# Which engine issues the first loads: the two heads of a unit from one DMA queue or from two

## The chip, the cores and the metric

The kernel runs on one core of one Trainium2 chip. A core has five engines with instruction streams of their own: TensorE (PE, matrix products; its weight loads are shown apart as PEld), VectorE (DVE), ScalarE (ACT), GpSimd (POOL) and SyncE (SP), which here only issues transfers. They meet through semaphores. Transfers between the memory of the chip and the core's working memory (SBUF) are done by 16 DMA engines; an engine's stream only issues them. What is measured is the device time of one execution in microseconds (us), and less is better. The kernel before was timed in twelve executions: median 558.64 us, from 556.56 to 561.17.

## The reference

Two blocks follow one another. The first is a gated linear recurrence over 768 tokens, for 4 batches and 8 heads of width 48; the second mixes tokens and channels with a Fourier transform, normalises, and puts a two-layer network on top:

```python
f = 1 / (1 + exp(-f_logit))
for t in range(S):                       # per batch and head
    state = f[t, :, None] * state + k[t, :, None] * v[t, None, :]
    y[t] = q[t] @ state
x = y with the heads side by side        # (4, 768, 384)
u = x + real(fft(fft(x, axis=tokens), axis=channels))
out = u + relu(layernorm(u) @ w_ch1) @ w_ch2      # 384 -> 1536 -> 384
```

The arrays q, k, v and f_logit are inputs in float32. The weights w_ch1 and w_ch2 come as float64, and the kernel makes single precision of them on the chip.

## The kernel before

**Units.** The recurrence is done for two heads at a time. Such a pair of heads of one batch is a *unit*; there are 16, numbered u = 0 to 15, four for each batch. The channels of the pair lie on the partitions: the first head (r = 0) on partitions 0 to 47, the second (r = 1) on 64 to 111, the 768 tokens along the free axis. The rows between are filled once by a memset (`gap` on DVE for q and k, line 131; `start` on POOL for g, lines 136 to 145). Three tiles g0 to g2 hold the gate logits in turn, three tiles k0 to k2 the keys, and four tiles q0 to q3 the queries, so unit 3 takes g0 and k0 again once unit 0 has read them.

**Loads.** `load(u, names)` (line 159) issues them. For each of f, k and q it issues two transfers of 48 rows with 3072 bytes each (144 KB), one for each head, second head first, at line 170, and for v one of 288 KB at line 166. All of these go out on SP. They, the weight blocks (`words`, line 267, 384 KB each, tile raw) and the identity matrix (line 872) stand in one queue in the order of the program. The framework gives every transfer one of eight completion semaphores in turn, so a transfer also waits until the one eight places before it has landed. A tile that is used again adds a wait for its readers.

**A unit's work** is cut into steps by the generator `attention` (lines 330 to 368) and `outputs` (506 to 566):

- ACT: exp and ln of the gate logits g, in place (330, 331)
- DVE: the running sum W of these (a scan, 337) and the sums at the chunk ends (338); POOL copies the last of them (339)
- ACT: g = exp(-W), W = exp(W), and te for the chunk ends (342 to 345)
- DVE: q times g, W times k (349, 350)
- PE: the scores sc (361); DVE masks them into at (368)
- PE turns W (506), ACT copies that to kT (508), PE makes the chunk states ds from kT and v (517), DVE scans them into stt (525)
- PE: y from at and v (537), and from q and stt (544); ACT copies y to yT (553 to 557), PE turns it (564), ACT writes x (566)

**Weights.** A block comes as pairs of words. ACT converts the low word in place (238), DVE shapes the high one (240, 241), and POOL adds the two (242).

**The order** is written out by hand in the string ORDER: a number is the next step of that unit, L2q a load, r the fetch of a weight block, C its conversion, G a gap memset, I and Z POOL's memsets, D four products on constant data on PE (line 153) that keep it busy. Each engine carries out its own part of this order, strictly in sequence. Later letters (F, P, H, W) are the Fourier transform and the network, which PE is full with from about 70 us on. The order begins:

```python
ORDER = (
    "Gq2 r I D Gq0 L0f Gk1 L1f D Gk0 L0q i D Gq3 C Gq1 Z L0k 0 D 1 Gk2 0 L1q 1 L1k D 0 0 1 0 r 1 L2f 0 2 "
    "C L1v 1 L3fk D 1 3 L0v 0 1 L2q 2 0 0 r D 1 L2k 3 1 0 2 r 3 L3q 2 L2v D 0 C L3v D C L4fk R D 4 2 2 3 "
```

So the load of unit 2's gate logits (L2f) stands behind several steps of units 0 and 1, and the first step of unit 2 follows it almost at once.

At the end of the kernel, behind a test that is not met with these inputs, stands a second, slower way through the whole computation; it calls `load` too.

Of the kernel before, what the change touches and what calls it, by code (L numbers as in the profile page):

```python
# [53 lines left out]
def kernel(  # L54
# [13 lines left out]
    nc = tc.nc  # L68
# [10 lines left out]
    ROWS = [slice(64 * r, 64 * r + D) for r in range(2)]  # L79
# [79 lines left out]
    def load(u, *names):  # L159
        if u >= B * HP:  # L160
            return
        b, hp = divmod(u, HP)
        for name in names:
            if name == "v":
                v_of[u] = p3.tile([128, NCH, 2 * D], F32, tag="v", name=f"v{u}")
                nc.sync.dma_start(out=v_of[u], in_=v[b, hp])
                continue
            t, i = {"f": (g_t[u % 3], 2), "k": (k_t[u % 3], 1), "q": (q_t[u % 4], 0)}[name]
            for r in (1, 0):
                nc.sync.dma_start(out=t[ROWS[r]], in_=qkf[b, hp, r, :, i])  # L170

    def tables():

# [201 lines left out]
    def attention_by_blocks(u, x_all):  # L375
# [114 lines left out]
        T = double(64, T)  # L490
        yield
        load(u + 3, "f")
        yield from outputs(u, x_all, AT, Q, K, None, T)
        load(u + 3, "k")

    def outputs(u, x_all, AT, Q, K, te, T=None):
# [61 lines left out]
        if te is None:  # L558
            load(u + 4, "q", "v")
# [415 lines left out]
```

## Time and profile before

| | us |
|---|---|
| median of twelve executions | 558.64 |
| lowest, highest | 556.56, 561.17 |
| the profiled execution | 558.71 |
| its span, first to last instruction | 556.9 |
| PE busy | 528.2 |
| DVE busy | 299.7 |
| ACT busy | 192.7 |
| POOL busy | 95.8 |

The profile is that of one execution. Times in it count from its first instruction, and 1.8 us of the execution's time lie around the span. "Chain" is the work that ended last, followed back from the last instruction: at each step to what released it. "Idle before" is the time in which an engine had nothing it could do ahead of an instruction, with what ended it. A load's issue is short (0.3 to 0.5 us on SP); the transfer itself lands microseconds later, which the trace shows in the increments of its completion semaphore. The TensorE clock is granted in steps; 1.00 is full speed.

### The profile page before, as it was taken

What the parts mean: (1) busy time and instruction counts of PE and PEld (TensorE: products, weight loads), DVE (VectorE), ACT (ScalarE), POOL (GpSimd) and SP (SyncE); (2) the same over time, 40 slices, a digit from 0 to 9 for tenths busy, and PEclk for the clock granted to TensorE, in tenths of its full rate; (3) what the DMA queues carried; (4) which work ended last, traced back from release to release, by engine and by line L of the source; (5) the groups of instructions that cost most, each with busy time, mean ns of one, the idle gap of its engine ahead of it and who ended that gap; (6) DMA issues with size and microseconds to landing.
All of it is one profiled execution on the core that took longest, in us unless ns stands there. A gap on an engine that the chain in (4) does not pass through costs nothing.

```text
span 556.9 us, 10217 instructions
## 1 busy us (share of the span) xinstructions
PE 528.2 (95%) x4194; PEld 462.9 (83%) x4194; DVE 299.7 (54%) x534; ACT 192.7 (35%) x497; POOL 95.8 (17%) x147
## 2 busy tenths in 40 slices
PE   3988599999999999999999999999999999999995
PEld 2877478885889889889889899899889798989985
DVE  8999899994945626445554443453443342413231
ACT  6766476573313433443240331321421302121110
POOL 6146642634101000140200000103001000010000
PEclk9698989999999999999999999999999999999999
DMA  8969736453402010310730401102012005000001
GB/s 223 261 184 234 204 92 172 128 146 105 115 1 58 15 44 2 115 44 22 220 114 15 114 1 55 32 1 87 1 28 86 0 2 171 0 29 0 29 2 34
DMA packets 18398, 44.38 MB, mean 80 GB/s; under 512 B 3109, under 2 KB 4710, under 8 KB 18342
## 3 DMA queue, kind: packets, MB, share of 16 engines
q1 hardware_dynamic: 17094, 39.89, 26.0%
q0 software_dynamic: 1104, 3.54, 1.8%
q8 instruction: 35, 0.57, 0.5%
q14 instruction: 21, 0.17, 0.1%
q10 hardware_dynamic: 144, 0.20, 0.1%
HBM read 38.90 MB, written 4.72 MB: 78 GB/s over the span
## 4 chain that ended last, share of the span: by engine, by line
PE 86%; DMA 5%; DVE 4%; ACT 2%; POOL 1%; issue 1%; SPq 0%; ACTq 0%; DVEq 0%; POOLq 0%
PE up L750 34%; PE fx L773 15%; PE fz L773 12%; PE z L650 4%; PE sc L361 3%; PE po L759 3%; PE mix L669 3%; PE y L537 3%; PE y L544 3%; DMA raw<-in_w_ch_dram 2%; DMA g<-in_qkf_dram 2%; PE ds L517 2%; PE pt L708 1%; PE yt L564 1%; DMA v<-in_v_dram 1%; PE st L506 1%
## 5 line engine op out<-in xcount | busy, mean ns | idle before, releaser
L750 PE MATMUL up<-unT,w 128*128 128x256 f32 x864 | 197.1, 382 | 1.5 <-DVE x L728 0.9
L750 PEld LDWEIGHTS up<-unT,w 128*128 128x128 f32 x864 | 160.9, 190 | 26.1 <-issue 1.5
L752 ACT ACTIVATE h<-up 128x256 f32<-128x256 f32 x144 | 55.2, 383 | 200.3 <-PE up L750 194.0
L617 POOL DMA_INDIRECT out_dram<-x,place x16 | 16.9, 1059 | 270.3 <-DVE x L803 234.4
L773 PE MATMUL fx<-block,h 128*128 128x192 f32 x264 | 46.5, 326 | 0.0
L773 PE MATMUL fx<-w,h 128*128 128x192 f32 x264 | 44.9, 327 | 0.1
L773 PEld LDWEIGHTS fx<-w,h 128*128 128x128 f32 x264 | 43.1, 190 | 0.8 <-ACT h L752 0.4
L773 PEld LDWEIGHTS fx<-block,h 128*128 128x128 f32 x264 | 43.5, 190 | 0.0
L780 DVE TENSOR_TENSOR s<-h,h 128x768 f32<-128x768 f32 x11 | 10.5, 954 | 50.6 <-ACT h L752 50.6
L242 POOL TENSOR_TENSOR w<-w,raw 128x384 uint32<-128x384 uint32 x24 | 28.9, 1210 | 50.6 <-ACT raw L238 24.1
L361 PE MATMUL sc<-q,W 48*64 48x128 f32 x768 | 28.5, 299 | 6.8 <-DVE W L350 5.3
L368 DVE COPY_PREDICATED at<-causal,sc 128x768 f32<-128x768 uint32 x32 | 31.5, 1029 | 3.4 <-PE sc L361 3.3
L361 PEld LDWEIGHTS sc<-q,W 48*64 48x64 f32 x768 | 24.2, 148 | 10.8 <-DVE W L350 5.8
L337 DVE TENSOR_TENSOR_SCAN W<-g,bound 112x768 f32<-112x768 f32 x16 | 28.4, 1775 | 1.3 <-PE st L506 0.9
L725 DVE TENSOR_TENSOR x<-mix,x 128x384 f32<-128x384 f32 x12 | 6.7, 555 | 39.4 <-PE mix L669 39.4
L537 PE MATMUL y<-at,v 128*64 128x128 f32 (+1 forms) x384 | 24.5, 276 | 0.0
L773 PE MATMUL fz<-w,s 128*128 128x192 f32 x132 | 23.5, 328 | 0.0
L773 PE MATMUL fz<-block,h 128*128 128x192 f32 x132 | 23.5, 328 | 0.0
L773 PE MATMUL fz<-w,h 128*128 128x192 f32 x132 | 23.4, 327 | 0.0
L537 PEld LDWEIGHTS y<-at,v 128*64 128x64 f32 (+1 forms) x384 | 20.9, 130 | 2.9 <-issue 2.8
L153 PE MATMUL y<-bound 128*128 128x256 bf16 x92 | 15.4, 318 | 8.1 <-ACT yT L557 4.2
L773 PEld LDWEIGHTS fz<-w,s 128*128 128x128 f32 x132 | 21.6, 190 | 0.3 <-issue 0.3
(145 smaller groups left out, 742.2 us busy)
## 6 DMA issues: line engine op xcount, KB each, us to landing
raw<-in_w_ch_dram SPq DMA_DIRECT2D x24, 384.0 KB, 4.3
g<-in_qkf_dram SPq DMA_DIRECT2D x32, 144.0 KB, 4.7
q<-in_qkf_dram SPq DMA_DIRECT2D x32, 144.0 KB, 4.8
k<-in_qkf_dram SPq DMA_DIRECT2D x32, 144.0 KB, 4.4
v<-in_v_dram SPq DMA_DIRECT2D x16, 288.0 KB, 5.4
k<-in_w_ch_dram SPq DMA_DIRECT2D x12, 384.0 KB
g<-in_w_ch_dram SPq DMA_DIRECT2D x12, 384.0 KB, 5.2
out_dram<-x SPq DMA_DIRECT2D x4, 168.0 KB
```

Of the source, the lines that this page charges most:

```text
L242: nc.gpsimd.tensor_tensor(bits, bits, lo, ALU.add)
L337: nc.vector.tensor_tensor_scan(W, g, bound[:R], 0.0, ALU.add, ALU.min)
L361: nc.tensor.matmul(ps[64 * s:64 * s + 64, r, i * C:(i + 1) * C], lhsT=W[ROWS[r], o + 64 * s:o + 64 * s + 64], rhs=Q[ROWS[r], o:o + C], sta ...
L368: nc.vector.copy_predicated(AT[:, :, half], causal.bitcast(U32).unsqueeze(1).unsqueeze(1).to_broadcast([128, 2, NCH // 2, C]), ps[:, :, :N ...
L537: nc.tensor.matmul(y[FILL[r], c * C:(c + 1) * C], lhsT=vt[:, c, r * D:r * D + (64 if r == 0 else D)], rhs=AT[:, r, c], start=(c % 4 == 0), ...
L544: nc.tensor.matmul(y[ROWS[r], c * C:(c + 1) * C], lhsT=st[ROWS[r], :, c - 1], rhs=Q[ROWS[r], c * C:(c + 1) * C], start=False, stop=True, s ...
L617: nc.gpsimd.indirect_dma_start(out=out.rearrange("b s d -> (b s) d"), out_offset=bass.IndirectOffsetOnAxis(ap=place[:, b, i:i + 1], axis=0 ...
L650: nc.tensor.matmul(z[:, cols], lhsT=src[:, j, lo:hi], rhs=tab[:, t, T % 2, cols], start=(i == 0), stop=(i == len(parts) - 1), skip_group_c ...
L669: nc.tensor.matmul(mix[:, o], lhsT=zz[:rows_of[T], T, PLACES[c]], rhs=cd[:rows_of[T], T, :NQ - odd], start=(i == 0), stop=(i == 1))
L750: nc.tensor.matmul(pp[:, :256], lhsT=w1[:, kt, m * 128:(m + 1) * 128], rhs=unT[:, kt], start=(kt == 0), stop=(kt == 2))
L752: nc.scalar.activation(hs[-1][:, m % H].rearrange("p t n -> p (t n)"), pp[:, :256], AF.Relu)
L773: nc.tensor.matmul(out, lhsT=h[:, m], rhs=blocks[i][:, m], start=(start and m == 0), stop=(m == H - 1), skip_group_check=True)
```

## The change

Of the two transfers that load f, k or q of a unit, the one for the first head (r = 0) is issued by ACT instead of SP, for the units 0, 1 and 2. For units 3 to 15 both stay with SP, as do v, the weights and the constants. These are nine transfers of 144 KB. They stand in ACT's instruction stream at the places where `load` is called in ORDER.

```diff
             t, i = {"f": (g_t[u % 3], 2), "k": (k_t[u % 3], 1), "q": (q_t[u % 4], 0)}[name]
             for r in (1, 0):
-                nc.sync.dma_start(out=t[ROWS[r]], in_=qkf[b, hp, r, :, i])
+                queue = nc.scalar if r == 0 and u < 3 else nc.sync
+                queue.dma_start(out=t[ROWS[r]], in_=qkf[b, hp, r, :, i])
```

## The prediction

> **What bounds the kernel now.** I read four views, in this order: the page's head, the chain that ended last, the timeline of ScalarE (ACT) where the moved loads will stand, and the sums by stage.
>
> ```profile
> span 556.9 us, 10217 instructions
> PE 528.2 (95%) x4194; PEld 462.9 (83%) x4194; DVE 299.7 (54%) x534; ACT 192.7 (35%) x497; POOL 95.8 (17%) x147
> q1 hardware_dynamic: 17094, 39.89, 26.0%
> q10 hardware_dynamic: 144, 0.20, 0.1%
> PE 86%; DMA 5%; DVE 4%; ACT 2%; POOL 1%; issue 1%; SPq 0%; ACTq 0%; DVEq 0%; POOLq 0%
> ```
>
> TensorE is the bound, but not of the stage that is changed. Its waits after 68 us are small; of the 28.7 us that it is idle, 19.5 lie before 70 us (sums by stage). q10 is ACT's DMA queue: 144 packets, one store at the very end. So no load runs beside SP's queue (q1) in this trace.
>
> The nine moved loads all go out in the first 17 us. The chain there:
>
> ```profile
> 0.81 4.16 DMA raw<-in_w_ch_dram
> 6.09 1.01 POOL w L242
> 7.10 2.63 POOL at L214 x2
> 10.94 0.71 POOL deep L339
> 11.67 0.84 ACT W L343
> ...
> 20.36 0.95 PE st L506 x5
> 21.39 1.77 DVE W L337
> ...
> 23.27 0.75 DVE stt L525
> 24.02 1.66 DVE W L337
> 25.90 0.85 ACT g L342
> ```
>
> It runs from the first weight block through POOL's fills to ACT and VectorE (DVE), and has no load of a unit in it between 5 and 41 us. What is late in these rows is late at 41 us too: the pieces follow one another with gaps of some 0.04 us. From 41.5 to 66 us it goes over SP's loads, which start when computing frees their tiles, and from 68.5 us over TensorE. I find no slack further on that would take a delay back.
>
> How tight the loads stand to their readers is seen on ACT and in the sums by stage (columns: stage, busy time by engine, granted clock, DMA share, GB/s):
>
> ```profile
> 14.47 0.48 ACT L345 ACTIVATE te<-deep,low 112x240 f32<-112x240 f32 x1
> 14.86 0.83 ACT L330 ACTIVATE g<-g 112x768 f32<-112x768 f32 x1
> 18.05 0.84 ACT L331 ACTIVATE g<-g 112x768 f32<-112x768 f32 x1
> 21.33 0.63 ACT L508 COPY kT<-st 128x560 f32<-128x560 f32 x1 [2.44 <-PE st L506]
> ```
>
> ```profile
> 2.00:3.00 1.00, 0.00 (x0) 0.00 (x0) 0.89 (x2) 0.10 (x1) 0.94 (x3) 1.00 0.72 160
> 3.00:4.00 1.00, 0.06 (x1) 0.07 (x2) 0.89 (x2) 0.00 (x0) 0.94 (x6) 1.00 1.09 390
> 5.00:10.00 5.00, 3.39 (x16) 2.11 (x14) 4.28 (x7) 4.10 (x8) 3.93 (x8) 1.00 1.05 262
> ```
>
> The DMA engines are full from 5 us on (share 1.05). The trace's completion increments put the landings of g0 at 5.45 and 6.01, of g1 at 6.57 and 7.09, of q0 at 7.53 and 8.15: one half head pair per 0.54 us, against an issue every 0.46 us on SP. The transfers set the pace, not SP. ACT reads g2 at 14.86, and its second half had landed at 14.72.
>
> **The change, part by part.** It removes nine DMA issues from SP and adds nine to ACT: the rows 0 to 47 of g, q and k for units 0, 1, 2. Bytes, tiles and all arithmetic stay. The order of TensorE, DVE and POOL is the same in both builds; ACT's becomes (r0 is the moved half):
>
> ```
> table load, g0 r0, g1 r0, q0 r0, raw0, k0 r0, exp/ln g0, exp/ln g1, q1 r0, k1 r0,
> exp W0 and te0, exp W1 and te1, g2 r0, exp/ln g2, raw1, exp/ln g3, kT0, kT1, q2 r0, k2 r0, exp W2 ...
> ```
>
> *SP loses nine issues*: 9 x 0.46 = 4.1 us of a queue that is ahead of the transfers; I take a gain of 0. The cover is the transfer pace; were it gone, 4.1 us would be the ceiling. What SP is moved past (k, raw1, g2's other half) starts sooner but has readers that need both halves or come much later (raw1's at 17.5 us). The loads of unit 3 still wait for DVE at 12.78.
>
> *g0, g1, q0 at the start.* On SP they stood at 1.75, 2.67 and 3.60. On ACT they follow the table load (0.81 to 2.09), so from about 2.1: no later. But they now move beside raw0, the head of the chain, instead of behind it. If raw0 keeps its precedence the cost is 0; if all three (432 KB) get ahead of it, 3 x 0.54 = 1.6 us. raw0's first packets ran 0.9 us after its issue, so ACT's begin near 3.0, when by the stage rows 0.18 of raw0's 0.39 MB has been moved. I assume even sharing of the rest: 0.21 MB more in between, at the 390 GB/s of that microsecond, 0.55 us. I take **+0.6** (0 to 1.6). g0's other half is late by about as much, and POOL, ACT and DVE with it.
>
> The Trainium skill speaks to this on "DMA: Bandwidth & Descriptors", section "Queues, rings and completion order": each DMA engine alternates between the rows that have work, a packet from each. By that rule the sum holds the 0.6; by first come, first served, it would hold 0. This trace shows no two load queues at once, so it can't say. The same page's section "Issuing engines are not separate DMA queues" speaks against any gain: a second issuing engine saves issue time alone.
>
> *k0, q1, k1.* k0 r0 goes out near 5.7 (SP: 5.53) and is read at 12.67: 0. q1 and k1 wait in ACT's queue behind ln g1 and go out between 8.8 and 10 instead of 6.89 and 7.71. Read at 13.66 and 14.60, they have 4 us or more, and loads issued then landed in 3.6 to 5.5. I take 0, at most 0.6. Their two issues stand ahead of exp W0's first half (9.99), whose successor waits for POOL until 11.67: 1.7 us of cover against 0.9.
>
> *g2, the costly one.* On SP its second half was issued at 9.20, on ACT it can't be before te1, that is 14.5 to 14.95, and its reader is the next instruction. ACT then waits for the whole flight. Flights of such a load: 2.60 is the shortest in the whole trace, the ones issued on SP around then took 3.6 to 4.8 (g at 12.78: 3.58; q at 15.00: 4.83). An empty queue of its own should beat SP's backlog; I take 3.7, landing at 18.65. Bounds: 14.47 + 2.60 = 17.1, 14.95 + 4.83 = 19.8. Queued behind this wait are exp and ln of g2, raw1, exp and ln of g3 (14.86 to 18.89: 4.03 us) and then kT0, which began at 21.33 because it waited for TensorE. So 2.44 us of ACT's idle time covers: kT0 begins at 18.65 + 4.03 = 22.7, **1.35 late** (0 to 2.5). kT0 is waited for by TensorE's ds (22.16), that by DVE's stt (23.27). From kT0's start to ds is 0.83, and ds takes 0.76 at full clock: ds ends at 24.3, stt starts **1.1 late** (0 to 2.2). Behind stt on DVE stands the scan of unit 3, behind that ACT's exponentials, yT and TensorE's next block at 29.05. DVE's scan of W2 (21.39) is not touched: ln g2 ends at 20.4. A raw1 that is converted late reaches POOL at 20.4 instead of 18.6; POOL is idle until 23.2.
>
> *q2, k2.* Issued on ACT after kT1, about 24, instead of 15.47 and 16.93; read at 26.45 and 27.30, now some 1.7 later. With 3.7 of flight they land near 27.7 and 28.1: 0; with the 5 to 8 us that SP's queue showed at that time, one to three late, but the scores that read them began at 30.08 behind yT, which covers 1.8. I take 0 (0 to 1.0). Their two issues, 0.9 us if ACT stops for them, lie ahead of exp W2, which has more cover than that from unit 3's scan.
>
> *The granted clock* is not the change's, but moves with it: TensorE runs at 0.50 from 12.27 to 22.51 and from 66.88 to 73.71, in steps of 3.41 us. One step more or less over full work is 3.41 x 0.5 = 1.7 us. I take 0 (-1.7 to +1.7).
>
> **Sum.** 0.6 + 1.1 = 1.7 us onto the profiled execution: 556.9 of span and 1.8 around it, 558.7, which is the median of the twelve runs (558.64) to 0.1. So **560.4 us**.
>
> **The rivals.**
> 1. *Hidden*: raw0 keeps its precedence, and g2 lands by 17.3 (flight 2.6 with an empty queue, issue run ahead of te1). Then kT0 is on time: **558.7**. For it: 2.44 us of cover on ACT, the shortest flight. Against it: DMA engines full until 30 us.
> 2. *Worse*: the flight is 4.8 or more because the engines are full, ACT stops for its issues, and q2/k2 come late as well: 1.6 + 2.2 + 0.9 = 4.7, **563.4**. For it: flights of 5 to 8 us on SP between 15.5 and 22. Against it: those queued behind SP's own raw blocks.
> 3. *Faster*: the clock. The work that meets 70.29 to 73.71 is TensorE's 3.42 us at half rate. If the shift puts the busy stretch so that one step fewer is slow, 1.7 us fall away; with a shift under 0.6 the result is **557.0 to 557.6**. It decides only where g2's wait is covered, too. For it: the step before it holds 1.78 us of work in 3.41, so not much is missing. Against it: a shift can as well lose a step.
> That SP's freed time brings the transfers forward is not among them: they are full, and the chain holds none of the first loads but raw0.
>
> **How the numbers follow.** My case 0.47, own range 559.8 to 562; hidden 0.24; worse 0.15; faster 0.14. The range goes from rival 3's upper end to just short of rival 2's full sum: **557.5 to 563.0**, which leaves half of either, some 0.15, outside. A measurement here tells 0.2% (1.1 us) from no change: faster 0.14, same 0.24, slower 0.62.
>
> **What would show it.** In the changed kernel's profile: q10 with nine loads more; on ACT a wait for DMA g at unit 2's exp, ending near 19, 3 to 4 us long, and none there would favour the first rival; raw0 landing near 5.5, not 4.97; kT0 near 23.2 and TensorE's block of 29.05 near 30.7; everything from 68 us on shifted alike. I am wrong if ACT's own queue flies in under 2.6 us, if a shift is there at 30 us and gone at 68, or if the clock's steps differ in number.

## The result and the profile after

The changed kernel takes 563.38 us (median of 12, from 560.37 to 565.35), the kernel before, timed beside it, 558.23 (49 executions). The ratio is 1.0084, with a 95% interval from 1.0067 to 1.0100: **slower by 4.7 us** (3.7 to 5.6). The forecast was slower, with 560.4 in a range from 557.5 to 563.0; the median lies 0.4 above that range, and 558.23 and the 4.7 of the ratio, 562.9, lie just inside it. One more execution on record, 567.12, is not among the twelve. The profiled execution took 563.63, 4.9 more than that of before.

From the page of the changed kernel:

```profile
span 561.4 us, 10216 instructions
PE 528.5 (94%) x4194; PEld 462.9 (82%) x4194; DVE 300.4 (54%) x534; ACT 192.8 (34%) x497; POOL 95.7 (17%) x147
q1 hardware_dynamic: 16518, 38.57, 25.3%
q10 hardware_dynamic: 720, 1.52, 1.2%
PE 83%; DMA 6%; DVE 4%; ACT 2%; POOL 2%; issue 1%; SPq 0%; DVEq 0%; ACTq 0%; POOLq 0%
```

576 packets, nine loads of 64, have gone from q1 to q10. No engine's busy time grows by more than 0.7 us (DVE); TensorE has become idle for longer, and the chain holds more DMA. Where, the chain shows, cut to its first 45 us (columns: start, length, what):

```profile
0.81 4.41 DMA raw<-in_w_ch_dram
...
12.00 0.84 ACT W L344
...
14.10 4.45 DMA g<-in_qkf_dram
18.58 0.94 ACT g L331 x2
...
21.78 0.85 ACT g L332
22.63 0.78 ACT kT L509 x2
23.45 7.59 DMA k<-in_qkf_dram
...
31.16 0.96 DVE W L351
32.12 0.28 DVE w L241
...
34.49 1.96 DVE at L369 x2
```

(The lines of the kernel are one higher than before.) Two transfers now stand in it that were not there: unit 2's gate logits, issued at 14.10, and its keys, issued at 23.45, each directly behind the ACT work that keeps the issue back. The timeline of ACT shows that:

```profile
14.05 0.84 ACT L344 ACTIVATE W<-W 112x768 f32<-112x768 f32 x1
14.10 0.38 ACTq L171 DMA_DIRECT2D g<-in_qkf_dram  x1
14.80 0.48 ACT L346 ACTIVATE te<-deep,low 112x240 f32<-112x240 f32 x1
18.58 0.84 ACT L331 ACTIVATE g<-g 112x768 f32<-112x768 f32 x1 [3.30 <-DMA g<-in_qkf_dram]
22.53 1.18 ACT L509 COPY kT<-st 128x560 f32<-128x560 f32 x2
23.09 0.32 ACTq L171 DMA_DIRECT2D q<-in_qkf_dram  x1
23.45 0.43 ACTq L171 DMA_DIRECT2D k<-in_qkf_dram  x1
```

ACT runs on while it issues: the load of g2 goes out while exp W1 is running. What costs is not the issue but its place. On DVE, first in the kernel before, then in the changed one:

```profile
26.45 0.93 DVE L349 TENSOR_TENSOR q<-q,g 112x768 f32<-112x768 f32 x1
27.30 0.95 DVE L350 TENSOR_TENSOR W<-W,k 112x768 f32<-112x768 f32 x1
...
29.42 0.56 DVE L241 SCALAR_TENSOR_TENSOR w<-raw,w 128x384 uint32<-128x384 uint32 x1
30.96 2.00 DVE L368 COPY_PREDICATED at<-causal,sc 128x768 f32<-128x768 uint32 x2 [0.99 <-PE sc L361]
```

```profile
14.76 0.96 DVE L350 TENSOR_TENSOR q<-q,g 112x768 f32<-112x768 f32 x1 [0.81 <-DMA q<-in_qkf_dram]
...
22.41 1.76 DVE L338 TENSOR_TENSOR_SCAN W<-g,bound 112x768 f32<-112x768 f32 x1 [0.86 <-PE st L507]
...
24.29 0.75 DVE L526 TENSOR_TENSOR_SCAN stt<-ds,te 112x288 f32<-112x288 f32 x1
...
29.48 0.96 DVE L350 TENSOR_TENSOR q<-q,g 112x768 f32<-112x768 f32 x1 [1.93 <-ACT W L344]
31.16 0.96 DVE L351 TENSOR_TENSOR W<-W,k 112x768 f32<-112x768 f32 x1 [0.73 <-ACT raw L239]
32.04 0.35 DVE L241 TENSOR_SCALAR w<-raw 128x384 uint32<-128x384 uint32 x1
...
33.30 1.27 DVE L242 SCALAR_TENSOR_TENSOR w<-raw,w 128x384 uint32<-128x384 uint32 x1
34.49 1.96 DVE L369 COPY_PREDICATED at<-causal,sc 128x768 f32<-128x768 uint32 x2
```

In the same profile, on POOL:

```profile
33.13 1.02 POOL L243 TENSOR_TENSOR w<-w,raw 128x384 uint32<-128x384 uint32 x1 [6.19 <-ACT g L331]
```

DVE first waits 0.81 us for q1 (the line at 14.76) and is some 1.0 us late from there to stt. Of unit 2, the two waits that are put down to ACT were ended by the loads: the completion counts have q2's first head landing at 29.40 and k2's at 31.04, each 0.1 us before the instruction that reads it. The mask is 3.53 us late, the next TensorE blocks up to 3.5 (the turning of W at 42.51 instead of 39.03), and TensorE's last product ends at 554.31 instead of 550.42, 3.89 late. The rest of the 4.9 us, 1.0, lies behind that last product, where nothing of the change runs: from there to the end of the execution it is 9.32 us (7.05 to the end of the span, 2.27 around the span), and 8.29 before.

The landings of the loads that matter, from the issues and completion counts of the trace:

```
                       before (SP)               after (ACT)
                 issued  landed  flight    issued  landed  flight
g2, first head     9.20   14.72    5.52     14.10   18.55    4.45
q2, first head    15.47   20.59    5.12     23.09   29.40    6.31
k2, first head    16.93   24.62    7.69     23.45   31.04    7.59
```

### The profile page after: what moved, and what is told of

It reads as the page before. It is cut to its first block, busy times and chain, and to the rows that moved or that the text cites. A ratio compares the mean times of both kernels' runs of the same rounds, so it can differ in the third digit from the quotient of the medians.

```text
span 561.4 us, 10216 instructions
## 1 busy us (share of the span) xinstructions
PE 528.5 (94%) x4194; PEld 462.9 (82%) x4194; DVE 300.4 (54%) x534; ACT 192.8 (34%) x497; POOL 95.7 (17%) x147
## 4 chain that ended last, share of the span: by engine, by line
PE 83%; DMA 6%; DVE 4%; ACT 2%; POOL 2%; issue 1%; SPq 0%; DVEq 0%; ACTq 0%; POOLq 0%
PE up L751 34%; PE fx L774 15%; PE fz L774 12%; PE z L651 4%; PE po L760 3%; PE mix L670 3%; PE y L545 2%; PE sc L362 2%; PE y L538 2%; DMA raw<-in_w_ch_dram 2%; DMA wave<-in_dim_tab_dram 2%; PE pt L709 1%; PE ds L518 1%; DMA k<-in_qkf_dram 1%; PE yt L565 1%
## 5 line engine op out<-in xcount | busy, mean ns | idle before, releaser
L545 PE MATMUL y<-q,stt 48*48 48x128 f32 x320 | 21.9, 281 | 0.0
```

What stands on the lines that cost most here:

```text
L545: nc.tensor.matmul(y[ROWS[r], c * C:(c + 1) * C], lhsT=st[ROWS[r], :, c - 1], rhs=Q[ROWS[r], c * C:(c + 1) * C], start=False, stop=True, s ...
```

## The experiments

All twelve kernels were timed in five rounds beside the kernel before, with twelve executions each, but seven of e9, ten of e10 and eleven of e12. The times below are the ratio times the time of before in the same set, with the 95% interval; a single profile is used for what waits for what. How far a single profile can stray is told under the last pair.

| kernel | moved to ACT | us against before |
|---|---|---|
| the change | all nine | +4.7 (3.7 to 5.6) |
| e1 | units 0 and 1 | +0.4 (-0.4 to 1.2) |
| e2 | g2 | +0.8 (-0.3 to 2.0) |
| e3 | q2, k2 | +0.4 (-0.4 to 1.2) |
| e4 | none; q2, k2 late on SP | +2.6 (1.3 to 3.8) |
| e5 | all nine, unit 2's early | +1.7 (0.7 to 2.6) |
| e6 | none; more filler on TensorE | -1.5 (-2.6 to -0.3) |
| e7 | g2, q2, k2 | +2.8 (1.7 to 3.9) |
| e8 | units 0, 1 and g2 | +2.1 (0.8 to 3.3) |
| e9 | units 0, 1 and q2, k2 | +4.7 (3.0 to 6.4) |
| e10 | all nine, v3 on SP later | +4.7 (3.2 to 6.2) |
| e11 | none; 18 in the way that is not taken | -0.3 (-1.2 to 0.5) |
| e12 | all nine, none in the way that is not taken | +3.6 (2.5 to 4.7) |

**e1, only the units 0 and 1.**

```diff
-                nc.sync.dma_start(out=t[ROWS[r]], in_=qkf[b, hp, r, :, i])
+                queue = nc.scalar if r == 0 and u < 2 else nc.sync
+                queue.dma_start(out=t[ROWS[r]], in_=qkf[b, hp, r, :, i])
```

> Only the six first-head loads of units 0 and 1 on ACT, unit 2 back on SP. Theory Late (a load costs what its issue comes later on ACT than on SP, as far as its reader has no cover): raw0 lands near 5.2, q1's first head is issued near 9.3 and lands near 14.6, unit 1's product is some 1.0 late and the stt of unit 0 with it; exp of g2 and the products of unit 2 wait for no load. Total +0.9 us (0.4 to 1.3). Theory Queue (a transfer on ACT's queue is slow or slows SP's, wherever it stands): two thirds of the 4.7, +3.1. Theory Hold (ACT itself stands still for each issue): up to 6 x 0.4, +2.4, with a gap of 0.4 on ACT at each issue.

Measured: 558.61, +0.4, not to be told from nothing. raw0 lands at 4.58 with three loads of ACT beside it; before it was 4.97, and in kernels without them 4.74 and 4.92 (e4, e3). So the loads beside raw0 don't hold it back, and six loads in a second queue cost little by themselves, 1.2 us at most.

**e2 and e3, unit 2's parts by themselves.**

```diff
+                queue = nc.scalar if r == 0 and u == 2 and name == "f" else nc.sync   # e2
+                queue = nc.scalar if r == 0 and u == 2 and name != "f" else nc.sync   # e3
```

> Only the first head of g2 on ACT, eight loads back on SP. Late: issued near 13.8, lands near 18.2, exp of g2 waits 3 to 4 us as in the changed kernel, stt of unit 0 is 0.7 to 1.0 late, unit 2's products wait for nothing else: +1.0 us (0.5 to 1.3). Queue: one ninth of 4.7, +0.5. Hold: +0.4.

> Only the first heads of q2 and k2 on ACT. Late: issued near 22.4 and 22.8 behind the two kT copies, landing near 28.5 and 29.5 to 30, W times k of unit 2 at some 29.7 instead of 27.3, of which 1.0 us is covered by DVE's idle time ahead of the mask: +1.2 to +2.2 us. Queue: two ninths of 4.7, +1.0. Hold: +0.8.

Measured: 558.01 and 558.13, +0.8 and +0.4, both compatible with nothing. That was the surprise: q2 and k2 go out at 22.37 and 22.79 in e3, hardly sooner than in the change. The waits of SP's queue, in e2 and then in e3, from 10 to 35 us, tell what else happened:

```profile
SPq L171 <- DMA g<-in_qkf_dram: 4.3, 1, 4.3
```

```profile
SPq L166 <- DMA q<-in_qkf_dram: 7.5, 2, 7.1
```

The loads take the completion semaphores in turn, over both queues. In e2, SP's load of q2 (second head) got the semaphore that ACT's late g2 had, and was held for 4.3 us, until g2 landed at 19.82. In e3, SP's load of v3 (288 KB) was held for 7.1 us behind q2, and SP issued nothing between 20.77 and 28.24. So nothing new of SP's came beside k2; its flight was 5.78 instead of 7.59, it landed at 28.57 instead of 31.04, and the mask came 1.5 us late instead of 3.5. The edit of a part had changed the order of the rest. e2's profile doesn't look like a kernel that loses 0.8: its mask is at 34.40, 3.44 late, on a chain that starts with g2. That execution took 561.60, where the twelve go from 556.79 to 561.83; more on this under the last pair.

**e4, the same lateness without ACT.** The loads of q2 and k2 (first head) stay on SP, but stand behind q3, v2 and v3 there. They go out at 20.77 and 22.33, some 1 to 2 us sooner than from ACT in the change, and land about as late, at 30.12 and 30.77.

```diff
-    "C L1v 1 L3fk D 1 3 L0v 0 1 L2q 2 0 0 r D 1 L2k 3 1 0 2 r 3 L3q 2 L2v D 0 C L3v D C L4fk R D 4 2 2 3 "
+    "C L1v 1 L3fk D 1 3 L0v 0 1 L2q 2 0 0 r D 1 L2k 3 1 0 2 r 3 L3q L2v L3v s2q s2k 2 D 0 C D C L4fk R D 4 2 2 3 "
...
+                late = n == 2 and word in ("L2q", "L2k")
+                load(n, *word.strip("L0123456789"), heads=(1,) if late else (1, 0))
+            elif kind == "s":
+                load(n, *word.strip("s0123456789"), heads=(0,))
```

> Nothing on ACT: all loads on SP, but the first heads of q2 and k2 stand behind q3, v2 and v3 in SP's queue, so that they are issued near 21 and 22. Late: they land near 29.2 and 29.7, behind everything issued before, and the cost is that of the kernel with both on ACT, +1.0 to +2.0 us. Queue and Hold: 0, since ACT issues nothing.

Measured: 560.09, +2.6. Its chain between 18 and 36 us:

```profile
20.77 9.35 DMA q<-in_qkf_dram
...
30.22 0.58 DVE q L349
...
31.09 0.96 DVE W L350
...
32.15 2.84 PE sc L361 x48
```

The mask is 3.44 late, as in the change, with not one load on ACT. So neither a second queue nor ACT's issuing is needed for this part of the loss: a late place in the order of the loads is enough.

**e5, all nine on ACT, but unit 2's earlier in ACT's order.**

```diff
-    "... L1q 1 L1k D 0 0 1 0 r 1 L2f 0 2 "
+    "... L1q 1 L1k a2f D 0 0 1 0 r 1 L2f a2q 0 2 a2k "
...
+            elif kind == "a":
+                load(n, *word.strip("a0123456789"), heads=(0,))
```

In this kernel the load of a first head goes to ACT for u < 3, as in the change.

> All nine first-head loads on ACT as in the changed kernel, but unit 2's stand further ahead in ACT's stream: g2 behind k1 (issue near 10), q2 ahead of exp g2 (near 14 to 15), k2 behind ln g2 (near 17). Late: g2 is there when exp g2 is reached, q2 and k2 land by 21 and 25, the wait at unit 2's products is gone; what is left is raw0 (+0.3) and q1 (+0.8): +0.5 to +1.2 us. Queue: +4.7, as the changed kernel. Hold: +3.6.

Measured: 560.39, +1.7 instead of +4.7. The three loads now go out at 9.62, 13.53 and 16.91, and the mask is 0.67 late. The nine loads on ACT's queue by themselves are not what costs; 1.7 is left, and of this the end of the kernel has about 0.9 (below).

Of the three theories that the expectations of e1 to e5 set against each other, Late (the loads go out late because of their place in the program) is the one that holds, by e4 and e5. Queue (two load queues are in each other's way) falls with e1, e4 and e5; Hold (the issues stop ACT's own work) falls with e1, e4 and the timeline of ACT above.

**e6, more filler on TensorE in the kernel before.** Five more words D stand ahead of the first scores, 20 products on constant data.

```diff
-    "... L0k 0 D 1 Gk2 0 L1q 1 L1k D 0 0 1 0 r 1 L2f 0 2 "
+    "... L0k 0 D 1 Gk2 0 L1q 1 L1k D D D D D D 0 0 1 0 r 1 L2f 0 2 "
```

> The kernel before with twenty more of TensorE's filler products (line 153) ahead of the first scores, all loads on SP. If the granted clock's step is worth what the prediction's third rival said, 1.7 us for 3.4 us of full work, the filler up to 12.8 takes the half-rate stretch of 12.27 to 22.51 away or shortens it, the scores of units 0 and 1 take 1.5 us each instead of 2.8, and 1 to 2.5 us fall away. If the stage is bound by DVE, which is busy in 0.97 of every microsecond from 8 to 19, it is 0 to -0.7 us.

Measured: 557.04, ratio 0.9973 (0.9953 to 0.9994), 1.5 us faster than before. It is the fastest of all kernels here. Granted clock (behind the busy times) from 12 to 23 us and in three later stretches, in before and in e6:

```profile
12.00:23.00 11.00, 9.28 (x130) 8.05 (x130) 9.93 (x11) 7.99 (x14) 1.02 (x1) 0.53 1.04 251
46.00:50.00 4.00, 3.82 (x55) 3.21 (x56) 3.05 (x6) 1.49 (x3) 1.77 (x2) 0.57 1.03 236
57.00:65.00 8.00, 5.09 (x90) 4.20 (x90) 5.62 (x10) 1.75 (x7) 4.20 (x8) 1.00 0.71 194
66.00:74.00 8.00, 6.10 (x42) 4.12 (x39) 7.62 (x16) 6.34 (x16) 5.74 (x13) 0.57 0.42 117
```

```profile
12.00:23.00 11.00, 8.06 (x153) 6.68 (x155) 10.25 (x13) 8.29 (x15) 1.21 (x2) 0.84 1.04 250
46.00:50.00 4.00, 4.00 (x72) 3.44 (x65) 3.68 (x7) 2.15 (x5) 2.21 (x3) 1.00 1.00 259
57.00:65.00 8.00, 6.98 (x83) 6.02 (x83) 5.61 (x12) 1.78 (x3) 3.35 (x7) 0.57 0.75 195
66.00:74.00 8.00, 6.80 (x59) 5.19 (x56) 7.69 (x15) 5.35 (x21) 5.79 (x10) 1.00 0.19 57
```

Less of the time is at half rate in this execution. That this is the cause of the 1.5 us isn't shown: e1 and e9 had full clock throughout 12 to 23 us and were no faster, and e11 below shows that the stretches move from execution to execution.

**e7 to e9: do the parts add up, or is g2 needed?** Unit 2 alone (e7), the change without q2 and k2 (e8), the change without g2 (e9).

```diff
+                queue = nc.scalar if r == 0 and u == 2 else nc.sync                                      # e7
+                queue = nc.scalar if r == 0 and (u < 2 or (u == 2 and name == "f")) else nc.sync         # e8
+                queue = nc.scalar if r == 0 and (u < 2 or (u == 2 and name != "f")) else nc.sync         # e9
```

> First heads of g2, q2 and k2 on ACT, units 0 and 1 wholly on SP. Theory Compound (g2's wait pushes the issue of q2 and k2 far enough back that they land behind v2 and v3, so that unit 2's three cost more together than g2 alone, +0.8, and q2 with k2, +0.4): +3 to +4.7 us, unit 2's W times k near 31. Theory Additive (each costs what it costs alone; the rest of the 4.7 is from elsewhere): +1.2 us (0.5 to 2.0).

> The changed kernel with the first heads of q2 and k2 back on SP: seven loads left on ACT. Compound: the wait at unit 2's products is gone, the one at exp g2 is left: +0.8 to +1.5 us. Additive: 4.7 less 0.4, +4.3 us.

> The changed kernel with the first head of g2 back on SP: eight loads left on ACT. Compound: exp g2 is on time or 0.5 late, q2 and k2 are issued near 22.4 and 22.8 and land near 28.3 and 29.5: +0.6 to +2.0 us. Additive: 4.7 less 0.8, +3.9 us.

Measured: 560.89, 560.82 and 563.12. e9 has the whole loss with g2 on SP, where ACT reads it at 15.53 and then waits 2.95 us for TensorE ahead of kT0: k2 lands at 30.70, the mask is 3.69 late. So g2's late issue isn't needed. Nor do the parts add: e9 is e1 and e3 together, +0.4 each, and costs 4.7; g2 is worth 0.8 by itself (e2) and nothing to be seen on top of q2 and k2 (the change against e9). So Compound falls with e9 (it set 2.0 as the most) and Additive with e8 (4.3 expected, 2.1 measured). By the profiles both delays meet at the same place, the mask of unit 2, and the later one counts. With q2 and k2 on SP (e8) the mask is at 31.47, and 2.6 us of the change's 4.7 are gone. In e7, v3 was held as in e3 and k2 landed at 28.94, yet the mask is 3.6 late: there g2 landed at 18.68 and its delay was the later one, and its chain runs from that landing over ACT, kT and TensorE to the scores at 33.70, with no k2 in it.

**e10, v3 behind the next loads.** e3 had escaped with v3 held back; here v3 is put further back by the order.

```diff
-    "... L3q 2 L2v D 0 C L3v D C L4fk R D 4 2 2 3 "
+    "... L3q 2 L2v D 0 C D C L4fk L3v R D 4 2 2 3 "
```

Otherwise it is the changed kernel.

> The changed kernel, all nine loads on ACT, with unit 3's v (288 KB on SP) moved behind g and k of unit 4 in SP's queue. In the changed kernel k2's first head and v3 were issued at 23.45 and 23.44 and landed at 31.04 and 31.34. If what stands in the DMA engines ahead of k2 makes its flight, k2 lands 0.5 to 1.0 earlier and +3.7 to +4.4 us are left of the 4.7; if ACT's own queue makes it, nothing changes.

Measured: 563.61, +4.7. k2 lands at 30.03, 1.0 sooner than in the change, and the mask is 2.5 late instead of 3.5. But k2 also went out 0.86 sooner, at 22.59, and its flight is 7.44 against 7.59. In e12 (below), which executes the loads of the change and leaves v3 in its place, k2 went out at 22.59 too and landed at 30.18. So hardly any of the gain is v3's. The way was not cleared either: the two loads of g4, 288 KB together like v3, now go out at 22.30 and 22.80 and land ahead of k2, at 29.07 and 29.87. What the transfers ahead of k2 cost it, e10 doesn't tell.

**e11 and e12: what makes the end longer?** The stretch behind TensorE's last product falls in two groups: 7.75 to 8.3 us in before, e1, e2, e3, e4, e6 and e7, and 9.0 to 9.4 in the change, e5, e8, e9 and e10, the kernels with seven and more moved loads (the text on record says eight and nine; e8 has seven). In it each engine reaches the test for the second way, and ACT's program has grown both ahead of that test and in the way that is not taken. e11 is the kernel before with 18 loads of that way on ACT; e12 is the change with the loads of that way left on SP.

```diff
+    def load(u, *names, again=False):
...
+                queue = nc.scalar if again and u < 3 else nc.sync                        # e11, otherwise before
+                queue = nc.scalar if r == 0 and u < 3 and not again else nc.sync         # e12
...
+            load(u, *("fkqv" if u < 3 else "qv"), again=True)
```

> The stretch behind TensorE's last product (to the end of the span, and what lies outside it) took about 8.1 us in before and in the kernels with up to six loads moved, except that one with eight moved loads and all with nine took 9.0 to 9.4. This kernel is the kernel before, but in the way that is not taken (the second computation behind the test on line 883, which runs only if the first result is unsafe) all 18 loads of the first three units' f, k and q stand on ScalarE: 18 instructions more in ScalarE's program, as the change has, and none of them is executed. Theory Length (the end is longer because ScalarE's program is longer, and its branch over the way not taken takes longer): TensorE's end as before, the stretch behind it 9.0 to 9.4, the time +0.9 to +1.3 us. Theory Work (the end is longer through what the moved loads did when they ran): the stretch 7.8 to 8.3, the time within 0.3 us of before.

> The changed kernel, but the loads of the way that is not taken stay on SyncE: all nine moved loads run as in the change, and ScalarE's program is nine instructions longer than before, not eighteen. Theory Length: the stretch behind TensorE's last product is 7.8 to 8.4 us (as with the kernels that have up to 14 instructions more, all but one), and the time is +3.6 us; the late landings (q2, k2 and g2) are as in the change and alone account for it. Theory Work: the stretch is 9.0 to 9.4 us and the time +4.7 us, as in the change.

Measured: e11 557.87, -0.3, with a stretch of 7.88 us; e12 561.83, +3.6, with 8.41. e11 refutes that the length of the untaken way by itself makes the end longer. e12 lies just above the bound set for that theory (8.4) and far from the 9.0 of the other. Neither fits. What does go with the stretch is q14, the queue of instruction fetches. Its packets in the profile's last stretch (545 to 566 us), for before, e11, e12 and the change:

```profile
q14 instruction: 6, 0.05, 0.9%
```

```profile
q14 instruction: 6, 0.05, 0.8%
```

```profile
q14 instruction: 7, 0.06, 1.0%
```

```profile
q14 instruction: 8, 0.07, 1.1%
```

Six in all kernels of the first group, seven in e8 and e12, eight in the change, e5, e9 and e10. The count alone doesn't give the stretch: with seven it is 9.14 in e8 and 8.41 in e12. ACT's branch at the test starts at 557.2 in the change and its next instruction at 560.4 (3.2 us; 2.7 in before, 3.0 in e12), and SP, which closes the program, has then to wait for it:

```profile
SPq L971 <- ACTq L884: 0.3, 1, 0.3
```

Of the 1.03 us between the two profiles, 0.43 lie in this branch and 0.46 outside the span. What lies outside the span is on record for every execution: 2.1 to 2.4 us in all of the change, 1.7 to 1.9 in those of before, 1.7 to 1.8 in e12. So the end costs about 1 us (9.2 against 8.1, the means of the two groups), and it goes, if not strictly, with fetches of instructions. What makes the end longer stays open. That the longer end explains the difference between e12 (+3.6) and the change (+4.7) fits in size, but the intervals of the two overlap.

e11 also gives the measure of a single profile: it executes the same instructions as before, yet TensorE's end is at 551.73 (before 550.42), and the clock is at half rate in other places (compare the rows of before under e6):

```profile
12.00:23.00 11.00, 9.22 (x134) 7.82 (x134) 9.95 (x12) 7.90 (x14) 1.06 (x2) 0.60 1.05 243
46.00:50.00 4.00, 4.00 (x82) 3.60 (x84) 3.65 (x8) 2.16 (x5) 1.78 (x2) 1.00 1.04 225
57.00:65.00 8.00, 6.37 (x77) 5.55 (x78) 5.64 (x11) 0.44 (x1) 3.38 (x6) 0.59 0.76 203
```

So 1.3 us at TensorE's end mean nothing between two single profiles. Its mask, at 30.71, is 0.25 from before's; the 3.5 of the change are far outside that. But kernels with late loads vary more. e12, which executes the loads of the change, has its mask 2.82 late. The profiles of e2 and e4, both with the mask 3.44 late, are of executions of 561.60 and 563.26, 3.6 and 3.2 above the medians of these kernels. So how late the mask is in one profile shows where the delay comes from, and doesn't price it: 2.5 late in e10 goes with +4.7, 2.8 in e12 with +3.6, 3.4 in e4 with +2.6 and in e2 with +0.8.

## Why the prediction was right in sign and short in size

The mechanism was right: loads that stand in ACT's program go out behind ACT's work, land late, and the delay is carried to the end (3.53 at unit 2's mask, 3.89 at TensorE's end). Wrong were sizes, and with them the place: the sum put its 1.7 on g2 and raw0, and most of the 4.7 comes through q2 and k2, which it had at 0.

| term of the sum | predicted | measured |
|---|---|---|
| the loads of units 0 and 1 (raw0 held up) | +0.6 | +0.4 (e1), raw0 not held up |
| g2 | +1.1 | +0.8 alone (e2), nothing beside late q2 and k2 |
| q2, k2 | 0, at most 1.0 | +2.6 (from e8 to the change; also e4) |
| the end of the kernel | not in the sum | about +1.0 |

The measured terms add to 4.8, or to 4.0 without g2's. They come from different kernels, each with an interval of about one microsecond to either side, and g2's depends on what else is late.

- **SP loses nine issues: 0.** Nothing contradicts it: e1 frees six of them and gains nothing. The page "DMA: Bandwidth & Descriptors" of the Trainium skill, section "Issuing engines are not separate DMA queues", says that starting transfers from several engines saves issue time alone. e1 agrees, with +0.4.
- **g0, g1 and q0 beside raw0: +0.6. Not borne out.** raw0 landed at 5.22 in the change, but at 4.58 and 4.64 in e1 and e5, which issue the same three loads at the same place, against 4.97 in before and 5.11 in e2, which don't. The difference goes either way. A reading was off too: raw0's first packets ran 1.05 after its issue, not 0.9.
- **k0, q1, k1: 0, at most 0.6. Wrong.** q1 landed at 14.64 and k1 at 15.53, past the 4 us of room that the text gave them; their flights were 5.35 and 5.88. W times k1 started 1.05 late (15.65 against 14.60), the scan of W2 1.02 (22.41 against 21.39), and stt, which stands right behind that scan, 1.02. In e9 k1 landed at 16.03, and stt is 1.54 late with g2 read in good time. In e1, where the two landed at 13.84 and 14.63, the same places are 0.24 to 0.38 late and the kernel is 0.4 slower. The error is of the same kind as the one of q2 and k2.
- **g2: right on ACT, and right at stt by coincidence.** It landed at 18.55 (18.65 forecast), ACT waited 3.30 (3 to 4), kT0 began at 22.53 and 1.20 late (1.35). The flight of 3.7 was 4.45, but the issue was sooner, beside exp W1 and not behind it. stt was 1.02 late (1.1), but not through g2: it followed DVE's scan without a gap, and that was late by q1. In e7, which leaves units 0 and 1 on SP, stt does wait for g2's chain, 0.83 for ds, and is 1.59 late. In the change the two delays run side by side, and only the later one counts.
- **q2 and k2: 0. This is the step that cost most**, and it failed in two places. First the flight. The text assumed 3.7 us since "an empty queue of its own should beat SP's backlog". It took 6.31 and 7.59, as long as SP's loads at that time and as k2's own on SP before (7.69). The landings came in the order of issue over both queues, but for a few tenths. So k2 landed 6.42 late; it had 2.68 of slack (24.62 to 27.30), and W times k2 started 3.86 late. Second the cover. The text had a case for flights of 5 to 8 us and put it at no cost, because the scores waited for yT and 1.8 were free there. That cover is real: the scores began 2.21 late, at 32.23. But the mask doesn't only wait for the scores. On DVE four instructions that shape weight words stand between W times k2 and the mask; DVE had 0.99 of idle time there, and that was all the cover: 2.87 of the 3.86 were left. The other 0.7 of the mask's 3.53 is the last of the four (the line at 33.30), which took 1.27 instead of 0.56, beside an addition on POOL that had begun 0.17 before it. It is as long (1.25 to 1.26) in e3, e4, e9, e10 and e12, each time with POOL's addition just ahead; in before POOL's began 0.20 after it. That POOL is the reason, no run shows. What is queued behind the late instruction on its own engine had been listed for ACT's wait for g2, and not for DVE's wait for k2.
- **The clock: 0.** In the two profiles of before and after the half rate takes the same number of steps (the text left out the one of before from 46.40 to 49.81), so nothing there speaks for a part of the difference. But e11 has other steps with the same executed work, so the profile of one execution can't tell whether an edit gains or loses one. The third rival, faster by a step, could never have been decided from the profile of before.
- **No slack further on.** Right: TensorE is 4.2 late at 74 us and 3.9 late at its end.
- **The end.** The prediction looked at the program only as far as the work goes. The last 9 us of the execution, in which the engines branch over the second way, were not thought of, although the diff puts loads into that way too.
- **The rivals.** "Worse" had named the right number, 563.4, with a flight of 4.8 and more from full DMA engines and late q2 and k2. Its working is not confirmed by that: it added 1.6 for raw0, which is 0, and 0.9 for ACT stopping at its issues, which it doesn't (14.10 against 14.05 above). "Hidden" fell with the flight.

Does ACT's queue get its turn? The page "DMA: Bandwidth & Descriptors" of the Trainium skill, section "Queues, rings and completion order", says that a DMA engine alternates between the queue rows that have work, a packet at a time. From 26 to 29 us in the changed kernel both queues have work:

```profile
q1 hardware_dynamic: 243, 0.53, 73.0%
q10 hardware_dynamic: 106, 0.24, 33.5%
```

ACT's queue does move beside SP's, with 106 of 349 packets. It isn't half here, and in the three microseconds before that, with ACT's loads issued at 23.09 and 23.45, q10 had 13 packets out of 304, the first at 25.55. In e12 it had 45 of the 64 packets from 26.0 to 26.5, so the share isn't a fixed one, and nothing here shows which DMA engine had work in both queues at a time. An own queue gave these loads a share, and no precedence.

## What to carry to other kernels

Before a load is moved to a busy engine's queue, write down where it will stand in that engine's program and put its landing at issue plus the flight that loads had in that stretch; with the DMA engines full, an empty queue of its own did not shorten the flights of q2 and k2 here (6.3 and 7.6 us, against 5.1 and 7.7 on SP before). Then take each reader that becomes late and list what stands behind it on its own engine: the free time before the next *consumer* is no cover if the same engine has other work in between. And an edit that puts loads on another engine also redistributes the completion semaphores: test a part of it alone only with an eye on which transfer now waits for which.

## What the runs showed that was not expected

- A transfer on SP waited for a load on ACT because both had the same completion semaphore: 4.3 us in e2, 7.1 us in e3. e3, in which SP then issued nothing for 7.5 us, lost less through late q2 and k2 than e4, in which SP went on (+0.4 against +2.6).
- ACT's issues of loads run ahead of its running work: g2's at 14.10 beside an activation from 14.05 to 14.89, g0's at 1.57 during the table load (0.81 to 2.10).
- The stretch behind the last product was 1 us longer in the kernels with seven to nine loads moved on both sides of the last branch, with one or two more instruction fetches (7 or 8 against 6). Why is open.
- Twenty products more on constant data made the kernel 1.5 us faster (e6, 0.9973; 0.3 to 2.6). Why is open.
